# Matmuls of a standing tile of zeros put in front of waiting matmul groups, in a fused attention and mixture-of-experts kernel

## The chip, the core and the metric

The kernel runs on one NeuronCore of a Trainium2 chip. The metric is the device time of one execution in microseconds (us). The engines are named as in the profile: PE is the matmul engine, PEld its weight loads, DVE the vector engine, ACT the scalar engine, POOL GpSimd, SP the engine whose queue issues most transfers. [...]

## The reference

Eight batches, eight heads, 576 positions, head width 64. An attention over 32 memory slots a head gives 4608 token rows of 512; each row then goes through the one expert of eight that its gate picks.

```python
a = softmax(phi)                                   # [B, H, 576, 32]
k_m = einsum('bhsm,bhsd->bhmd', a, k)
v_m = einsum('bhsm,bhsd->bhmd', a, v)
attn = softmax(q @ k_m.T / sqrt(64))
x = (attn @ v_m).transpose(0, 2, 1, 3).reshape(4608, 512)
logits = x @ w_gate
e_idx = argmax(logits); gate_w = softmax(logits)[e_idx]
eom = sigmoid(x @ w_output_gate)
for e in range(8):
    m = e_idx == e
    out[m] = gate_w[m] * eom[m, e] * (relu(x[m] @ w1[e]) @ w2[e])
```

## The kernel before

The attention goes over four pairs of batches (`bp`), and within a pair over five groups of query columns; together 20 groups `g`, worked off in a software pipeline of steps `t`. The list `ORDER` fixes in which order the pieces of a step are written, and every engine runs its own pieces in that order. For a group, PE makes the scores (`scores`, L837, 16 matmuls), DVE transposes them (L847) and takes the maximum (L854), POOL subtracts it (L856), ACT takes the exponential (L860), DVE sums, POOL divides, DVE transposes back (L885), and three steps later PE makes the values (`values`, L898, in two halves of 8 matmuls, called V0 and V1 here; in the last group of a pair there is one half), which ACT copies out (L900, tile `xo`) and SP stores.

Between these pieces lies the work on the memories of the next pair, written out in the lists `MEM0` and `MEM`: transposes of the softmaxed phi (L702), sums of keys and values over positions (L731, tile `pk`, opened and closed by a matmul of a 1-row tile of zeros, L725 and L737), a scaled copy by ACT (L748, `kvm`), its transposes by PE (`turn_kv`, L757), and gates (L771).

When the groups of a pair are done, their tokens are ranked by expert (`rank`): PE adds up ones in a bank of PSUM (tile `pr`, L996 to L1002) that DVE reads (L1005). After the second pair, `route_early` gives the first experts their slots of 576 tokens: a long chain of small DVE operations ends in a comparison (`eqa`, L231), PE turns that into a table of token numbers (`table`, L241, 72 matmuls), DVE copies it out (L248) and makes indices, and POOL gathers the tokens of the first slot (L440, five gathers). Each use of `pr` is a new tile of a pool with one buffer.

Scores and values share the pool `pd` with two buffers of two banks each (tiles `bpd`). A tile that takes a buffer over waits for the last reader of the tile that held it.

The first slot opens in step 17 of the attention: `turn_x` transposes the gathered rows (L1134 in groups of four, L1139 for the last 64 rows), ACT and DVE split them into a high and a low part, and from L1306 on PE works through the experts' products. The rest of the attention is spread over the first two slots. A queue, an order and a buffer for each of these places are fixed when the program is built, except which expert a slot holds.

Of the kernel before, what the change touches and what calls it, by code (L numbers as in the profile page):

```python
# [7 lines left out]
F32 = mybir.dt.float32  # L8
# [45 lines left out]
GROW = ((4, 0, 0), (2, 0, 0), (0, 2, 0))  # L54
SOON = {"pe": 5, "dve": 3, "tab": 20}
PACE = 30
PUMP = (2, 1)
TURN = (12, 14, 16, 17)
TURN6 = (2, 3, 5, 8)
# [23 lines left out]
def attention_moe(tc, phiT, kv, qT, wgo, wall, out):  # L83
# [3 lines left out]
    with contextlib.ExitStack() as ctx:  # L87
# [42 lines left out]
        def iota_f(shape, pattern, base=0, cm=0, name="", dt=F32):  # L130
# [3 lines left out]
            if len(pattern) > 1:  # L134
# [8 lines left out]
                    for nm, n in (("a", NBE), ("l", NBL))}  # L143
# [21 lines left out]
        G.affine_select(out=upto[:], in_=upto[:], pattern=[[1, E], [-1, E]], base=0,  # L165
                        channel_multiplier=0, compare_op=ALU.is_ge, fill=0.0)
        wg = cp.tile([P, H, 16], F32, name="wg")

        ohg = rt.tile([P, NCHT, E], BF16, name="ohg", bufs=1)
        jh = rt.tile([P, NCHT], I32, name="jh", bufs=1)  # L170
# [51 lines left out]
        def table(nm, q, nch, nblk):  # L222
# [11 lines left out]
            yield  # L234
            yield from take_pr()
            yield from hold(LATE["pe"], SOON["tab"])
            pi = ps_r.tile([P, NBL], F32, name="pr")
            for c in range(nch):
                for i in range(2):
                    for r in range(2):  # L240
# [445 lines left out]
        def memory(bp):  # L686
# [65 lines left out]
                                hmask[:].unsqueeze(1).unsqueeze(3).to_broadcast(h2), ALU.mult)  # L752

            def turn_kv(b):
                pt = bank([2, P])
                for g in range(2):
                    T.transpose(pt[:, g], z[b]["kv"][:, g], ident[:])  # L757
                n = 2 * bp + b
                kT = kTp[n % 4]
                z[b]["vT"] = ld.tile([P, 2, P], F32, name="vT_b", bufs=1)  # L760
                for e in range(2):
                    A.copy(kT[64 * e:64 * e + 64], pt[0:64, e].rearrange("p (j m) -> p j m", m=M))
                A.copy(z[b]["vT"][64:128], pt[64:128])
                kTs[n] = kT
# [137 lines left out]
        def rank(bp, lg):  # L902
# [86 lines left out]
            def main():  # L989
                yield from take_pr()  # L990
                yield from hold(LATE["pe"], SOON["pe"])

                route = {1: route_early, NBP - 1: route_late}.get(bp)
                pr = ps_r.tile([P, NCH + 1, E], F32, name="pr")
                if route:
                    T.matmul(pr[:, NCH], ones_b[:], ohcs[bp][:], start=True, stop=True)  # L996
                T.matmul(pr[:, 0:NCH], strict[:], oh, start=True, stop=False)
                if bp:
                    T.matmul(pr[:, 0:NCH], ones_b[:], ohcs[bp - 1][:].unsqueeze(1).to_broadcast(b3),
                             start=False, stop=False)  # L1000
                for c in range(1, NCH):
                    T.matmul(pr[:, c:NCH], ones_b[:], oh[:, 0:NCH - c], start=False, stop=(c == NCH - 1))  # L1002
                yield
                yield from hold(LATE["dve"], SOON["dve"])
                V.tensor_tensor(w1_[:], oh, pr[:, 0:NCH], ALU.mult)  # L1005
                route = route(pr[:, NCH]) if route else iter(())
                next(route, None)
                taken.clear()
                yield
                yield from together(place(), route)  # L1010
# [60 lines left out]
        def turn_x(z, c):  # L1071
# [62 lines left out]
                T.transpose(pt[:, k * P:(k + 1) * P], xg[:, k, c * XQ:c * XQ + P], ident[:])  # L1134
            part(pt, (slice(None), c, slice(0, 512)))
            if c == 0:
                pt = bank([4, 64], "ps")
                for e in range(4):
                    T.transpose(pt[:, e], xg[0:64, 4, e * XQ:e * XQ + P], ident[0:64, 0:64])  # L1139
# [22 lines left out]
        def attention():  # L1162
# [8 lines left out]
            for t in range(NT + LAG["V"]):  # L1171
                for w in ORDER:
# [12 lines left out]
                    elif w == "V0" and 0 <= g < NT:  # L1185
# [3 lines left out]
                        if g == 5 * bp:  # L1189
                            lgs[bp] = rt.tile([P, NCH, 16], F32, name="lg", bufs=2)  # L1190
                        xo = wk.tile([P, 2, 2, 2 * XQ], F32, name="xo", bufs=2)
                        values(bp, 2 * c, st[g], xo)
                    elif w == "V1" and 0 <= g < NT:
                        if c < 4:
                            values(bp, 2 * c + 1, st[g], xo)
                        store(bp, c, xo, lgs[bp])
                    elif w == "C" and 0 < g < NT:
                        while 2 * (g // 5) + (g % 5 >= 2) not in kTs:
                            mem.step()
                        st[g] = scores(g // 5, g % 5)  # L1200
                        if g + NQ < NT:
                            load_q(g + NQ)
# [430 lines left out]
```

## Time and profile before

| | us |
|---|---|
| median of 3 runs | 544.62 (543.31 to 545.51) |
| the profiled execution, its own time | 544.71 |
| its span, first to last instruction | 543.0 |
| PE busy in the span | 503.2 (93%) |
| DVE busy | 370.4 (68%) |
| mean granted clock of PE | 0.953 |

A timeline row gives the start in us from the beginning of the span, the duration, the engine, the line, the operation with output and inputs, the shape, and the number of instructions merged into the row; where the engine was idle ahead of the row, the idle time and what ended it stand in brackets. [...] PE counts as busy while any matmul is under way, at whatever clock.

### The profile page before, as it was taken

The page shows a single profiled execution, that of the slowest core. Times are in us where ns is not written, and L with a number is a line of the kernel's source. Part 1 is how long each engine was busy: PE and PEld are TensorE (multiplying, and loading weights), DVE is VectorE, ACT ScalarE, POOL GpSimd, SP SyncE. Part 2 cuts the span into 40 slices and gives each one's busy share as a digit, 9 for nine tenths or more (in the row PEclk, how much of TensorE's full clock was granted, in tenths as well). Part 3 has the DMA queues.
Part 4 walks back from the last instruction along what each step waited for, and adds up shares of the span by engine and source line. Part 5 has one row for each costly group of instructions (what it writes and reads, how often), then busy time and mean ns, then how long its engine had stood idle before and what let it go on. Part 6 is the DMA issues. An engine that isn't in the chain of part 4 may idle for free. (4 is left out here: it accounts for less than half of the span.)

```text
span 543.0 us, 11086 instructions
## 1 busy us (share of the span) xinstructions
PE 503.2 (93%) x4205; PEld 431.6 (79%) x4205; DVE 370.4 (68%) x804; ACT 282.4 (52%) x543; POOL 170.0 (31%) x176
## 2 busy tenths in 40 slices
PE   3788797849999999999999999999999999999994
PEld 2455565539987799889988998998899899889983
DVE  4374979945982488826484898678779867977600
ACT  4476665254553454225353856576485657648311
POOL 2242645545151151115028223401621241131021
PEclk9977969868999999999999999999999999999998
DMA  8999999795454485217414951880496088120011
GB/s 333 412 397 384 412 385 353 258 344 182 180 167 155 139 235 198 77 73 272 139 37 136 264 174 36 271 244 33 149 263 173 30 267 246 43 94 34 0 45 49
DMA packets 46975, 104.31 MB, mean 192 GB/s; under 512 B 9856, under 2 KB 21440, under 8 KB 46528
## 3 DMA queue, kind: packets, MB, share of 16 engines
q1 hardware_dynamic: 41024, 83.44, 46.5%
q0 software_dynamic: 5888, 20.06, 11.0%
q8 instruction: 35, 0.57, 0.4%
q14 instruction: 28, 0.23, 0.1%
HBM read 77.23 MB, written 20.35 MB: 180 GB/s over the span
## 5 line engine op out<-in xcount | busy, mean ns | idle before, releaser
L1437 PE MATMUL bps<-whl,hh 128*128 128x512 f32 x560 | 167.3, 392 | 0.0
L541 DVE TENSOR_TENSOR whl<-w,whl 128x1024 fp32r<-128x1024 f32 x74 | 90.7, 1234 | 53.4 <-ACT whl L536 52.9
L1437 PEld LDWEIGHTS bps<-whl,hh 128*128 128x128 f32 x560 | 104.5, 188 | 22.0
L1437 PE MATMUL bps<-whl,hl 128*128 128x512 f32 x216 | 84.2, 390 | 0.0
L1306 PE MATMUL bps<-xh,whl 128*128 128x288 f32 x384 | 79.8, 299 | 0.0
L536 ACT CAST whl<-w 128x1024 fp32r<-128x1024 f32 x74 | 76.8, 1049 | 4.1 <-PE bpc L1437 2.7
L1306 PEld LDWEIGHTS bps<-xh,whl 128*128 128x128 f32 x384 | 62.9, 190 | 1.2 <-issue 0.6
L1265 POOL DMA_INDIRECT out<-y,idx_oa x20 | 26.3, 1316 | 102.8 <-ACT y L1264 75.1
L1306 PE MATMUL bps<-xl,whl 128*128 128x288 f32 x192 | 57.0, 297 | 0.0
L1265 POOL DMA_INDIRECT out<-y,idx_ol x20 | 22.3, 1113 | 101.1 <-ACT y L1264 66.6
L1334 PE MATMUL bpc<-xh,whl 128*128 128x288 f32 x240 | 49.5, 295 | 0.0
L1334 PE MATMUL bpc<-th,whl 128*128 128x288 f32 x240 | 49.2, 296 | 0.0
L1437 PEld LDWEIGHTS bps<-whl,hl 128*128 128x128 f32 x216 | 40.6, 188 | 8.1
L1264 ACT ACTIVATE y<-bps,gx 128x512 f32<-128x512 f32 x27 | 18.6, 690 | 44.3 <-PE bps L1437 43.5
L1274 ACT ACTIVATE hh<-bps 128x288 fp32r<-128x288 f32 x48 | 19.7, 411 | 40.4 <-PE bps L1306 40.3
L1334 PEld LDWEIGHTS bpc<-xh,whl 128*128 128x128 f32 x240 | 39.1, 188 | 0.2
L1334 PEld LDWEIGHTS bpc<-th,whl 128*128 128x128 f32 x240 | 38.7, 188 | 0.0
L1274 ACT ACTIVATE hh<-keep 128x288 fp32r<-128x288 f32 x60 | 26.3, 445 | 23.4 <-DVE keep L1345 23.4
L856 POOL TENSOR_TENSOR ea<-ea,mx 128x512 f32<-128x512 f32 (+1 forms) x20 | 19.3, 964 | 58.0 <-DVE mx L854 54.7
L1306 PEld LDWEIGHTS bps<-xl,whl 128*128 128x128 f32 x192 | 36.5, 190 | 0.1
L1334 PE MATMUL bpc<-xl,whl 128*128 128x288 f32 x120 | 35.4, 295 | 0.0
L1334 PE MATMUL bpc<-tl,whl 128*128 128x288 f32 x120 | 35.0, 292 | 0.0
(260 smaller groups left out, 935.0 us busy)
## 6 DMA issues: line engine op xcount, KB each, us to landing
w<-wall SPq DMA_DIRECT2D x64, 512.0 KB, 4.9
kvt<-kv SPq DMA_DIRECT2D x32, 512.0 KB, 7.4
xs<-xo SPq DMA_DIRECT2D x16, 576.0 KB, 6.4
qt<-qT SPq DMA_DIRECT2D x16, 512.0 KB, 9.2
ph<-phiT SPq DMA_DIRECT2D x3, 1152.0 KB, 11.5
xq<-xg SPq DMA_DIRECT2D x40, 80.0 KB, 4.9
xq<-xg SPq DMA_DIRECT2D x40, 64.0 KB, 4.3
kv<-kv SPq DMA_DIRECT2D x4, 512.0 KB, 9.2
```

Of the source, the lines that this page charges most:

```text
L536: A.copy(hl[:, 0], w[:])
L541: V.tensor_tensor(hl[:, 1], w[:], hl[:, 0].bitcast(F32), ALU.subtract)
L856: G.tensor_tensor(eav, eav, mx[:, 0:n].unsqueeze(2).to_broadcast([P, n, M]), ALU.subtract)
L1264: A.activation(y[0:n], py[0:n], AF.Copy, scale=z["g"][0:n, k:k + 1])
L1265: G.indirect_dma_start(out=out, out_offset=bass.IndirectOffsetOnAxis(ap=z["idx"][1][0:n, z["q0"] + k:z["q0"] + k + 1], axis=0), in_=y[0:n] ...
L1274: A.activation(h_[:, j, c:e], src, AF.Relu)
L1306: T.matmul(pb, w[:, b, o:o + P], x[a][:, cc, c * SL // 2:(c + 1) * SL // 2], start=(n == 0), stop=(n == 11))
L1334: T.matmul(pb, w[:, b, o:o + P], z[x][a][:, kc], start=(first and n == 0), stop=(n == 5), skip_group_check=not first)
L1437: T.matmul(py, a, w[:, b, DM * f:DM * f + DM], start=(u == 4 and f == 0 and n == 0), stop=(u == 7 and f == 1 and n == len(ps) - 1))
```

## The change

A tile `still` of 128 x 256 zeros in bf16 is set once by POOL. The function `keep` puts a number of matmuls of it into the second half of the bank that holds the ranks and tables; nothing reads what they write. To that end this bank becomes one standing tile `prs`, of which the ranks and tables use the first columns. `keep` is called ahead of scores (2 matmuls), of each half of the values (1), of the ranks (2), of the table (4) and of the transposes of `kvm` (3), as long as the first slot hasn't opened, and once ahead of L1139 in the first slot (6). The numbers stand in `KEEP`. One hundred such matmuls are issued, each with a weight load of its own.

```diff
--- before.py
+++ after.py
@@ -54,6 +54,7 @@
 GROW = ((4, 0, 0), (2, 0, 0), (0, 2, 0))
 SOON = {"pe": 5, "dve": 3, "tab": 20}
 PACE = 30
+KEEP = {"C": 2, "V": 1, "pr": 2, "tab": 4, "t": 3, "x": 6}
 PUMP = (2, 1)
 TURN = (12, 14, 16, 17)
 TURN6 = (2, 3, 5, 8)
@@ -165,6 +166,14 @@
         G.affine_select(out=upto[:], in_=upto[:], pattern=[[1, E], [-1, E]], base=0,
                         channel_multiplier=0, compare_op=ALU.is_ge, fill=0.0)
         wg = cp.tile([P, H, 16], F32, name="wg")
+        still = rt.tile([P, 256], BF16, name="still", bufs=1)
+        G.memset(still[:], 0.0)
+        prs = ps_r.tile([P, 512], F32, name="prs")
+
+        def keep(key):
+            if "open" not in env or key == "x":
+                for _ in range(KEEP[key]):
+                    T.matmul(prs[:, 256:512], ones_b[:], still[:], start=True, stop=True)
 
         ohg = rt.tile([P, NCHT, E], BF16, name="ohg", bufs=1)
         jh = rt.tile([P, NCHT], I32, name="jh", bufs=1)
@@ -234,7 +243,8 @@
             yield
             yield from take_pr()
             yield from hold(LATE["pe"], SOON["tab"])
-            pi = ps_r.tile([P, NBL], F32, name="pr")
+            pi = prs[:, 0:NBL]
+            keep("tab")
             for c in range(nch):
                 for i in range(2):
                     for r in range(2):
@@ -752,6 +762,7 @@
                                 hmask[:].unsqueeze(1).unsqueeze(3).to_broadcast(h2), ALU.mult)
 
             def turn_kv(b):
+                keep("t")
                 pt = bank([2, P])
                 for g in range(2):
                     T.transpose(pt[:, g], z[b]["kv"][:, g], ident[:])
@@ -991,7 +1002,8 @@
                 yield from hold(LATE["pe"], SOON["pe"])
 
                 route = {1: route_early, NBP - 1: route_late}.get(bp)
-                pr = ps_r.tile([P, NCH + 1, E], F32, name="pr")
+                pr = prs[:, 0:(NCH + 1) * E].rearrange("p (c e) -> p c e", e=E)
+                keep("pr")
                 if route:
                     T.matmul(pr[:, NCH], ones_b[:], ohcs[bp][:], start=True, stop=True)
                 T.matmul(pr[:, 0:NCH], strict[:], oh, start=True, stop=False)
@@ -1134,6 +1146,8 @@
                 T.transpose(pt[:, k * P:(k + 1) * P], xg[:, k, c * XQ:c * XQ + P], ident[:])
             part(pt, (slice(None), c, slice(0, 512)))
             if c == 0:
+                if z["s"] == 0:
+                    keep("x")
                 pt = bank([4, 64], "ps")
                 for e in range(4):
                     T.transpose(pt[:, e], xg[0:64, 4, e * XQ:e * XQ + P], ident[0:64, 0:64])
@@ -1189,14 +1203,17 @@
                         if g == 5 * bp:
                             lgs[bp] = rt.tile([P, NCH, 16], F32, name="lg", bufs=2)
                         xo = wk.tile([P, 2, 2, 2 * XQ], F32, name="xo", bufs=2)
+                        keep("V")
                         values(bp, 2 * c, st[g], xo)
                     elif w == "V1" and 0 <= g < NT:
+                        keep("V")
                         if c < 4:
                             values(bp, 2 * c + 1, st[g], xo)
                         store(bp, c, xo, lgs[bp])
                     elif w == "C" and 0 < g < NT:
                         while 2 * (g // 5) + (g % 5 >= 2) not in kTs:
                             mem.step()
+                        keep("C")
                         st[g] = scores(g // 5, g % 5)
                         if g + NQ < NT:
                             load_q(g + NQ)
```

The order on DVE, ACT and SP is the same in both kernels, and POOL has one more memset. On PE the matmuls are put in between; line numbers after the change are up to 17 higher. The rows below are of PE, from the scores of group 14 on, the last of the third pair (32x64): V0 and V1 of group 11 (each a row of one matmul and a row of three; a row with a wait stands alone), and the sums that follow, up to `pk`. In brackets stand the semaphores waited for, by the engine or the queue that raises them.

Before:

```order
L837 MATMUL bpd<-qt,kT_177 32x64 [waits DMAHW3_49,Activation_49]
L837 MATMUL bpd<-qt,kT_177 32x64 x7
L837 MATMUL bpd<-qt,kT_178 32x64 x8
L898 MATMUL bpd<-ve_b,aT 128x144 [waits DVE_49,Activation_49]
L898 MATMUL bpd<-ve_b,aT 128x144 x3
L898 MATMUL bpd<-ve_b,aT 128x144 [waits Activation_49]
L898 MATMUL bpd<-ve_b,aT 128x144 x3
L725 LDWEIGHTS zero
L725 MATMUL pk<-zero 128x256
```

After:

```order
L848 MATMUL bpd<-qt,kT_180 32x64 [waits DMAHW3_49,Activation_49]
L848 MATMUL bpd<-qt,kT_180 32x64 x7
L848 MATMUL bpd<-qt,kT_181 32x64 x8
L176 LDWEIGHTS ones_b
L176 MATMUL prs<-still,ones_b 128x256
L909 MATMUL bpd<-ve_b,aT 128x144 [waits Activation_49]
L909 MATMUL bpd<-ve_b,aT 128x144 x3
L176 LDWEIGHTS ones_b
L176 MATMUL prs<-still,ones_b 128x256
L909 MATMUL bpd<-ve_b,aT 128x144 [waits DVE_49]
L909 MATMUL bpd<-ve_b,aT 128x144 x3
L735 LDWEIGHTS zero
```

Two things moved. Each group has its matmuls of `still` in front. And V1, the second row with a wait, which waited for ACT (the copy out of V0, whose buffer it took over), now waits for DVE: the pool hands it the other buffer, the one that holds the scores at the head of the rows, and it waits for DVE to have transposed them (L847 before, L858 now). This is the only `bpd` tile of 56 whose buffer differs.

Where that transpose stands on DVE is seen in the rows of DVE after the change; before it they are the same, with the lines L231, L847, L854, L1040, L866, L868, L885 and L248:

```order
L240 TENSOR_TENSOR eqa<-iota_ba,q_1587 128x720 [waits DVE_49]
L858 STREAM_TRANSPOSE ea_186<-bpd 128x8x32 [waits PE_49]
L865 TENSOR_REDUCE mx<-ea_186 128x8 [waits DVE_49]
L1052 TENSOR_REDUCE lg<-xo 128x32 [waits Activation_49]
L877 TENSOR_REDUCE sa<-ea_185 128x16 [waits Activation_49]
L879 RECIPROCAL sa<-sa 128x16 [waits DVE_49]
L896 STREAM_TRANSPOSE aT<-ea_184 128x512 [waits Pool_49]
L258 COPY iv<-prs 128x20 [waits PE_49]
```

The transpose of those scores comes right behind `eqa`, the end of the routing chain, and the copy of the table (`iv`) six rows later; nothing moved here.

The six matmuls of `still` in the first slot stand between the first four transposes (L1134, now L1146) and L1139 (now L1153), which waits for DVE. Besides, the first matmul of `still` behind each reading of the bank by DVE waits for that reading: once after the ranks of the first pair, once after those of the second and once after the table.

## Rows read from the trace of the kernel before

**Rows 1.** Busy time by stretch: start:end, length, engines, granted clock, DMA share, GB/s.

```profile
45.00:51.80 6.80, 6.72 (x96) 4.62 (x96) 2.89 (x7) 3.43 (x9) 1.62 (x2) 0.50 1.00 386
68.80:79.10 10.30, 9.95 (x138) 6.48 (x134) 8.19 (x27) 6.13 (x15) 4.61 (x6) 0.50 1.05 399
79.10:102.20 23.10, 17.39 (x334) 11.92 (x332) 21.29 (x67) 12.36 (x29) 11.52 (x14) 0.93 0.88 296
113.20:126.90 13.70, 10.56 (x79) 8.65 (x80) 8.31 (x14) 8.18 (x18) 4.86 (x6) 0.50 0.68 243
126.90:536.00 409.10, 408.88 (x2654) 367.04 (x2652) 283.44 (x572) 214.36 (x389) 115.25 (x95) 1.00 0.48 144
420.00:430.00 10.00, 10.00 (x46) 8.29 (x45) 8.23 (x12) 7.77 (x12) 1.09 (x2) 1.00 0.06 13
```

**Rows 2.** Timeline of DVE: start, duration, operation; in brackets idle before, releaser.

```profile
52.81 0.72 DVE L847 STREAM_TRANSPOSE ea<-bpd 128x512 f32<-128x512 f32 x1 [3.29 <-PE bpd L837]
...
80.06 0.72 DVE L847 STREAM_TRANSPOSE ea<-bpd 128x512 f32<-128x512 f32 x1 [2.28 <-PE bpd L837]
```

**Rows 3.** Timeline of PE, 43 to 88 us, the same columns.

```profile
43.72 0.64 PE L731 MATMUL pk<-kvt,at 128*32 128x128 f32 x16 [0.64 <-DMA kvt<-kv]
...
65.48 0.46 PE L837 MATMUL bpd<-qt,kT 64*32 64x64 f32 x32 [0.50 <-ACT xo L900]
...
68.31 0.86 PE L898 MATMUL bpd<-ve_b,aT 64*128 64x144 f32 x8 [0.95 <-DVE ea L847]
69.10 0.39 PE L725 MATMUL pk<-zero 1*128 1x256 bf16 x1
69.42 1.94 PE L731 MATMUL pk<-kvt,at 128*32 128x128 f32 x32
...
72.33 1.38 PE L837 MATMUL bpd<-qt,kT 64*32 64x256 f32 x16 [0.35 <-ACT kT L762]
...
74.99 2.29 PE L898 MATMUL bpd<-ve_b,aT 64*128 64x144 f32 x16
...
80.33 1.26 PE L898 MATMUL bpd<-ve_b,aT 64*128 64x144 f32 x16
...
85.91 0.28 PE L725 MATMUL pk<-zero 1*128 1x256 bf16 x1
86.12 1.08 PE L731 MATMUL pk<-kvt,at 128*32 128x128 f32 x32
87.13 0.66 PE L837 MATMUL bpd<-qt,kT 64*32 64x256 f32 x16
```

**Rows 4.** Timeline of DVE, 100 to 105 us.

```profile
100.90 0.91 DVE L231 TENSOR_TENSOR eqa<-iota_ba,q 128x720 bf16<-128x720 bf16 x1
101.72 0.44 DVE L847 STREAM_TRANSPOSE ea<-bpd 128x256 f32<-128x256 f32 x1
...
104.29 0.14 DVE L248 COPY iv<-pr 128x20 f32<-128x20 f32 x1
```

**Rows 5.** Timeline of PE, 97 to 104 us.

```profile
97.79 0.76 PE L898 MATMUL bpd<-ve_b,aT 64*128 64x144 f32 x8 [0.78 <-ACT xo L900]
...
99.70 0.44 PE L757 MATMUL bpa<-ident,kvm 128*128 128x128 f32 x2
101.86 1.36 PE L241 MATMUL pr<-eqa,Aw 128*64 128x20 bf16 x72 [1.72 <-DVE eqa L231]
```

**Rows 6.** Timeline of POOL, 105 to 113 us.

```profile
105.31 1.24 POOL L440 DMA_INDIRECT xg<-xs,idx_ga  x1 [0.32 <-DVE idx_oa L255]
...
111.77 1.06 POOL L856 TENSOR_TENSOR ea<-ea,mx 128x512 f32<-128x512 f32 x1
```

**Rows 7.** Timeline of PE, 113 to 125 us.

```profile
114.47 2.29 PE L898 MATMUL bpd<-ve_b,aT 64*128 64x144 f32 x16
...
121.57 0.68 PE L1139 MATMUL bps<-ident,xg 64*128 64x64 f32 x4 [2.54 <-DVE ea L847]
122.18 2.83 PE L1134 MATMUL bps<-ident,xg 128*128 128x128 f32 x12
```

## The prediction

> **What bounds the kernel now.** I read the busy time by stretch first. From 126.9 us to 536.0, PE is busy 408.88 of 409.10 us at a granted clock of 1.00 [rows 1]: whatever moves the first slot's experts moves the end by as much, and nothing behind 126.9 is touched by the change. So the question is when the first slot gets to its products, and what is worth reading are the stretches ahead of it in which the clock stood at 0.50: 45.0 to 51.8, 68.8 to 79.1 and 113.2 to 126.9 [rows 1] (an earlier one and two shorter ones I leave aside: what PE does before 43.7 is overtaken by a wait for `kvt` [rows 3], and around the short ones DVE sets the pace).
>
> A slow PE costs something only where another engine waits for it. The timeline of DVE shows two such places behind the first two stretches: at 52.81 DVE had waited 3.29 us for scores, at 80.06 another 2.28 [rows 2]. Between 79.1 and 102.2 DVE is busy 21.29 of 23.10 us [rows 1]: there DVE sets the pace, a faster or slower PE changes little, but a chain that enters earlier leaves earlier. It ends with `eqa` (100.90, 0.91 long) [rows 4], the table on PE (101.86, 1.36) [rows 5], its copy on DVE (104.29) [rows 4], and five gathers that hold POOL from 105.31 to 111.77, where the next piece of the attention had stood behind them [rows 6]. Then values at half clock (2.29 us for 16), L1139 after a wait of 2.54 for DVE, twelve transposes in 2.83 [rows 7], and the experts.
>
> **What one matmul of zeros costs.** The trace has no run of them, but two neighbours. A bf16 matmul of 256 columns with its own weights (L725) takes 0.32 us until the next start at half clock (69.10 to 69.42) and 0.21 at full (85.91 to 86.12) [rows 3]; these stand alone. Back to back, 46 matmuls of 512 columns take 10.00 us [rows 1], 0.22 each, so half as many columns 0.11 at full and 0.22 at half clock. The new ones come in ones to fours: I take 0.15 and 0.27, with 0.11 to 0.21 and 0.22 to 0.32 as ends. In a wait that is there anyway they cost nothing.
>
> **Part by part.**
>
> *45 to 52 us.* What the clock is worth: the sums take 1.94 us against 1.08, the values 2.29 against 1.26, the scores 1.38 against 0.66 [rows 3]. This stretch holds one of each kind, so a held clock gives back 0.86 + 1.03 + 0.72 = 2.6. Nine new matmuls stand in it; two fit the wait for `kT` ahead of the scores (0.35 at the same place of the next pair [rows 3]); seven cost 1.05 at full clock, 1.9 at half. Ends: -1.6 if held, +1.9 if not. Before the clock fell at 45, PE waited for chunks of `kvt` (0.64 at 43.72 [rows 3], another just ahead), and no new matmul stands in front of those sums. I take a fall that is shorter than before and pays for the added ones: 0.
>
> *65 to 80 us.* The same pieces with the sums twice: 0.86 more, 3.5, less 1.05 gives 2.4; DVE can use no more than its wait, 2.28 [rows 2]. Ends -2.3 and +1.9. Ahead of the fall at 68.8 PE waited 0.50 at 65.48 and 0.95 at 68.31 [rows 3], and here the new matmuls stand right in front of the groups that waited, five of them and two with the ranks. I take a held clock: -2.3.
>
> [...]
>
> *The second half of the values of group 11.* It ran at 97.79 [rows 5]; now it waits for the transpose of the scores behind `eqa`, which ends at 101.72 + 0.44 = 102.16 [rows 4], and the table stands behind it on PE. Until the table is done PE has to make these 8 matmuls, L725, the sums, three matmuls of zeros, two transposes, four more of zeros, and the table. All at full clock that is 0.63 + 0.21 + 1.08 + 1.05 + 0.44 + 1.36 = 4.8 us [rows 3, 5]; all at half, with everything doubled that has no row, 1.15 + 0.32 + 1.94 + 1.9 + 0.9 + 2.7 = 8.9. PE has nothing to do for some 4 us ahead of it, so I take half clock for the first three (3.4) and full for the rest (2.85): the table ends at 108.4. DVE, which got to the copy at 104.29 [rows 4], copies 0.1 later. So the gathers, and all that stands behind them on POOL, come 4.2 us later against the chain; ends +2.7 and +6.9. It is hidden only if the gathers are not what the first slot waits for; POOL's next piece started as they ended [rows 6], so I count it whole. The two waits of matmuls of zeros for a reading of the bank cost less: the one after the second pair's ranks delays the values of group 10, but that lies in front of the same 4 idle us.
>
> *Values at 114.* At full clock 1.0 less for 2.29 [rows 7], less two matmuls of zeros: ends -0.7 and +0.5. PE waits before them for POOL and ACT, longer than before, with three new matmuls as only cover: 0.
>
> *The first slot.* The six cost nothing in a wait of 2.54 [rows 7] (6 x 0.27 = 1.6); if the wait shrinks, up to 1.6. Held, the clock would halve the 3.5 us of transposes and the 2.2 us of products until 126.9: -2.8; but each transpose goes through ACT and DVE before its product, so -1.6 is what I call the most, 0 the least. I take -0.8.
>
> [...]
>
> *Nothing else.* The memset of POOL lies in the first microseconds; DVE, ACT and SP keep their order.
>
> **Sum.** 0 - 2.3 + 4.2 + 0 - 0.8 = +1.1 us. The profiled execution took 544.71 us, 0.1 above the median; 545.8. A change under 0.5%, 2.7 us, is about what a measurement of this kernel can't tell from none.
>
> **Rivals.**
> - *The clock holds everywhere* (faster): also through 45 to 52 and around the table, values and first slot. -1.6 - 2.3 + 2.7 - 0.7 - 1.6 = -3.5: 541.2. For it: each of the three stretches ends with PE working without a pause, so a little more work may end them sooner. Against it: the 4 us without work ahead of 102, where no matmul of zeros stands.
> - *The clock still falls at 68.8* (slower): the term of 65 to 80 turns from -2.3 into +1.9: 550.0. It decides at the scores at 72: if these take 1.4 us again and not 0.7, this case is there. For it: a matmul of zeros is short beside waits of 0.95.
> - *The late table is hidden*: the first slot waits for ACT and stores instead, and the term of 4.2 is gone: -3.1, 541.6. Against it: POOL [rows 6].
>
> **Chances.** My sum 0.42 (543.3 to 547.6 alone), clock everywhere 0.27, clock falling at 68.8 0.23, hidden table 0.08. The runs before spread over 2.2 us, and the same holds after, so the cases overlap the bound of 2.7 us. Faster by over 0.5%: most of the first and third rival, 0.28; slower: most of the second and the upper part of mine, 0.27; within: 0.45. The range takes in both sides: 540.5 to 550.3.
>
> **What the profile after would show.** V1 of group 11 waiting for DVE some 4 us, and the table starting some 5 us behind the end of `eqa` where it now starts at once; the granted clock at 1.00 between 65 and 80, and DVE's wait of 2.28 gone; gathers some 2 us later than 105.31; the clock at 0.50 again around 102; the products starting at about 126. Wrong would be the prediction if the front gained more than 3 us ahead of `eqa`, if the table's delay were not found at the first slot's start, or if PE had waits behind 130.

## The result

The changed kernel took 550.5 us in the median (548.3, 550.06, 550.95 and 553.59), the kernel before 544.77 on the same chip: a ratio of 1.0109 with an interval of 1.0064 to 1.0154, so 5.9 us slower. The prediction was 545.8 with a range to 550.3. The profiled execution is the fastest of the four (span 546.5 us against 543.0, mean granted clock, as a share of full speed, 0.976 against 0.953), so the profile holds less than the whole loss.

The busy time of the changed kernel by stretch answers [rows 1]; the columns are the same (PE, PEld, DVE, ACT, POOL, granted clock, DMA share, GB/s).

```profile
35.50:45.00 9.50, 8.57 (x170) 5.82 (x168) 6.06 (x13) 6.72 (x14) 3.92 (x5) 1.00 0.92 313
45.00:51.80 6.80, 6.58 (x127) 4.22 (x127) 2.89 (x7) 3.81 (x11) 1.62 (x2) 1.00 0.99 364
68.80:79.10 10.30, 10.17 (x189) 6.76 (x189) 9.37 (x32) 7.69 (x19) 4.50 (x6) 1.00 1.03 406
79.10:93.00 13.90, 11.37 (x192) 7.15 (x192) 12.85 (x36) 7.42 (x17) 8.02 (x12) 1.00 1.02 360
93.20:100.00 6.80, 6.34 (x73) 4.20 (x72) 6.66 (x31) 2.38 (x5) 3.69 (x4) 0.50 1.00 332
110.20:117.00 6.80, 6.13 (x63) 3.37 (x63) 1.05 (x3) 2.43 (x5) 3.66 (x5) 0.50 0.88 333
123.90:127.30 3.40, 3.27 (x17) 3.16 (x18) 2.69 (x7) 1.54 (x3) 1.05 (x1) 0.50 0.54 204
127.30:543.60 416.30, 410.86 (x2662) 368.45 (x2661) 284.34 (x574) 215.06 (x390) 117.84 (x97) 1.00 0.47 142
```

In this execution the clock stood at 1.00 from 35.5 to 93 us, and of the three stretches at 0.50 that the prediction read, the first two are gone. The kernel is slower all the same. DVE, the timeline that answers [rows 2, 4]:

```profile
52.55 0.72 DVE L858 STREAM_TRANSPOSE ea<-bpd 128x512 f32<-128x512 f32 x1 [1.82 <-PE bpd L848]
78.86 0.72 DVE L858 STREAM_TRANSPOSE ea<-bpd 128x512 f32<-128x512 f32 x1 [0.72 <-PE bpd L848]
...
93.39 0.21 DVE L210 TENSOR_TENSOR tge<-prs,thr 128x64 f32<-128x64 f32 x1
...
99.75 0.91 DVE L240 TENSOR_TENSOR eqa<-iota_ba,q 128x720 bf16<-128x720 bf16 x1
100.58 0.44 DVE L858 STREAM_TRANSPOSE ea<-bpd 128x256 f32<-128x256 f32 x1
105.75 0.18 DVE L258 COPY iv<-prs 128x20 f32<-128x20 f32 x1 [2.53 <-PE prs L176]
```

`eqa` comes 1.15 us earlier than in [rows 4], but the copy of the table, which followed it there without a wait, comes 1.46 later, behind a wait of 2.53 for PE. PE in the same stretch and up to the first slot (answers [rows 3, 5, 7]):

```profile
45.09 0.65 PE L741 MATMUL pk<-kvt,at 128*32 128x128 f32 x16 [0.89 <-DMA kvt<-kv]
...
70.97 1.08 PE L741 MATMUL pk<-kvt,at 128*32 128x128 f32 x32
71.98 0.50 PE L176 MATMUL prs<-still,ones_b 128*128 128x256 bf16 x3
72.32 0.38 PE L768 MATMUL bpa<-ident,kvm 128*128 128x128 f32 x2
...
93.66 0.37 PE L176 MATMUL prs<-still,ones_b 128*128 128x256 bf16 x1 [2.35 <-DVE tge L210]
93.96 1.33 PE L909 MATMUL bpd<-ve_b,aT 64*128 64x144 f32 x8
...
101.08 0.76 PE L909 MATMUL bpd<-ve_b,aT 64*128 64x144 f32 x8 [0.66 <-DVE ea L858]
...
104.08 1.31 PE L251 MATMUL prs<-eqa,Aw 128*64 128x20 bf16 x72
...
108.99 0.25 PE L782 MATMUL bpa<-wg,vT_b 64*32 64x16 f32 x9 [1.94 <-issue]
...
113.74 1.01 PE L741 MATMUL pk<-kvt,at 128*32 128x128 f32 x10 [0.67 <-issue]
...
117.56 0.76 PE L909 MATMUL bpd<-ve_b,aT 64*128 64x144 f32 x8
...
124.03 0.69 PE L1153 MATMUL bps<-ident,xg 64*128 64x64 f32 x4 [2.40 <-DVE ea L858]
124.64 2.80 PE L1146 MATMUL bps<-ident,xg 128*128 128x128 f32 x12
127.12 0.46 PE L1323 MATMUL bps<-xh,whl 128*128 128x288 f32 x1
```

The first product of the kernel before, to hold against the last row:

```profile
124.66 0.59 PE L1306 MATMUL bps<-xh,whl 128*128 128x288 f32 x1
```

Read from the top of PE's rows: the sums of the second pair start 1.4 us later than at 43.72 in [rows 3], since PE's work in front of them has grown and their chunks of `kvt` come later. Then the sums take 1.08 instead of 1.94 us. Three matmuls of zeros take 0.34 until the next start. At 93.66 one matmul of zeros holds PE for 2.35 us until DVE has read the ranks, and the clock falls to 0.50 there. V1 of group 11 stands behind the transpose of the scores that follows `eqa` and starts at 101.08 instead of 97.79 [rows 5]; the table starts 3.42 us behind the end of `eqa` (100.66), where before it started at once. POOL's first gather (answers [rows 6]):

```profile
106.43 1.24 POOL L450 DMA_INDIRECT xg<-xs,idx_ga  x1 [2.59 <-DVE idx_oa L265]
...
112.88 1.05 POOL L867 TENSOR_TENSOR ea<-ea,mx 128x512 f32<-128x512 f32 x1
```

The gathers come 1.1 later, the first slot's small transposes 2.46 (124.03 against 121.57), its first product too (127.12 against 124.66).

The 3.5 us between the two profiled executions divide so. The end of `eqa` gives back 1.15. The first gather starts 5.77 us behind that end, where it stood at 3.50 [rows 4, 6]: 2.27 lost. From the first gather to the first product are 20.69 us against 19.35: 1.34 more. Behind the first product come another 1.0; the prediction wanted to see no waits of PE behind 130 us, and the trace after has two there, of 0.4 and 0.3 us.

### The profile page after: what moved, and what is told of

It reads as the page before. It is cut to its first block, busy times and chain, and to the rows that moved or that the text cites. A ratio compares the mean times of both kernels' runs of the same rounds, so it can differ in the third digit from the quotient of the medians.

```text
span 546.5 us, 11285 instructions
## 1 busy us (share of the span) xinstructions
PE 511.8 (94%) x4305; PEld 434.4 (79%) x4305; DVE 368.7 (67%) x804; ACT 282.4 (52%) x543; POOL 171.0 (31%) x177
## 5 line engine op out<-in xcount | busy, mean ns | idle before, releaser
L1323 PE MATMUL bps<-xh,whl 128*128 128x288 f32 x384 | 79.1, 297 | 0.0
L911 ACT COPY xo<-bpd 128x576 f32<-128x576 f32 x36 | 22.9, 639 | 31.6 <-issue 12.6
```

What stands on the lines that cost most here:

```text
L911: A.copy(xo[:, c % 2], px[:, :, 0:2 * XQ])
L1323: T.matmul(pb, w[:, b, o:o + P], x[a][:, cc, c * SL // 2:(c + 1) * SL // 2], start=(n == 0), stop=(n == 11))
```

## The experiments

My theory after the trace was: the late table is the loss, by the moved bank of group 11. Rivals: the wait for `tge`, the matmuls themselves, what they cost ahead of 45 us. Eighteen runs of seventeen kernels follow, each timed beside the kernel before on the same chip; the ratios go by that.

**By place.** `keep` gets the place as a number, and a table `WHERE` says where matmuls are issued; a key that isn't in it keeps all its places.

```diff
-        def keep(key):
-            if "open" not in env or key == "x":
+        def keep(key, n=0):
+            if ("open" not in env or key == "x") and n in WHERE.get(key, ANY):
...
-                        keep("V")
+                        keep("V", 2 * g + int(w[1]))
```

The number is the group for C, twice the group and the half for V, the pair of batches for pr, and the batch for t. The table of each run stands ahead of what was expected of it.

No zeros at all:

```diff
+WHERE = {"t": (), "C": (), "V": (), "pr": (), "tab": (), "x": ()}
```

> No matmul of zeros is issued anywhere; what stays is the one standing tile for ranks and tables, the tile of zeros and its memset. PE's order of matmuls is that of before, but the second half of the values of group 11 still takes the other double bank, so it still waits for the transpose behind eqa. Theory A (the buffer that the standing tile moves is part of the loss): the table starts 1.5 to 2.5 us behind the end of eqa instead of at once, gathers 1.5 to 2.5 us later, 546.3 to 547.3 us. Rival B (all of the loss is the matmuls of zeros themselves, at their places): 544.8 us, that of before, within 0.7. Rival C (the moved buffer is the whole loss): 549 to 551 us.

The front, up to 43 us:

```diff
+WHERE = {"t": (0, 1), "C": (1, 2, 3, 4), "V": (0, 1, 2, 3), "pr": (), "tab": (), "x": ()}
```

> The matmuls of zeros up to 40 us alone (23 of 100). Theory A: the chunks of kvt of the second pair are asked for 1.3 us later (as in the trace after), PE is 1.4 to 1.7 us late at 43.7, and this is overtaken by DVE's wait for scores at 52.8 only if the clock also comes back; here the clock falls at 45 as before, so about 1.5 us reach the ranks of the second pair: 1 to 1.5 us over the kernel with no zeros, 547.5 to 548.5. Rival B (what the front loses is swallowed by the waits of DVE between 52 and 80): the time of the kernel with no zeros, within 0.7.

The middle, 45 to 88 us:

```diff
+WHERE = {"t": (2, 3, 4, 5), "C": range(5, 14), "V": range(4, 20), "pr": (0,), "tab": (), "x": ()}
```

> The matmuls of zeros from 45 to 88 us alone (44 of 100), where in the trace after the clock stood at 1.00 and the shift of PE went from +2.6 to -1.5. Theory A (the gain in the middle is real and only paid away by what stands ahead and behind): eqa ends 1.5 to 3 us earlier than 101.8, the time is 1.5 to 3 us under the kernel with no zeros: 543.5 to 545.5. Rival B (the clock of the middle came from zeros further ahead, or the gain is taken by DVE's pace): the clock falls in 68 to 79 as before, the time is that of the kernel with no zeros plus up to 2 us.

Late, from the second pair's ranks on:

```diff
+WHERE = {"t": (6, 7), "C": range(14, 99), "V": range(20, 99), "pr": (1,)}
```

> The matmuls of zeros from the ranks of the second pair to the first slot alone (33 of 100). Theory A (half of the loss is made here: the matmuls around the table and PE's wait on its own issue at 107 to 109): 2 to 4 us over the kernel with no zeros, 548.5 to 551. Rival B (the wait on issue depends on how many instructions PE has had before, so it is gone when the first 67 are left out): under 1.5 us over the kernel with no zeros, with no wait on issue over 0.5 us in PE between 100 and 120.

Measured: none 1.0002 (0.9982 to 1.0021), front 1.0025 (1.0004 to 1.0047), middle 1.0006 (0.9983 to 1.0028), late 1.0086 (1.0063 to 1.0109). The tables issue 18, 48 and 34 matmuls; the 23, 44 and 33 in the expectations are miscounted. What was expected of the banks in the run without zeros was mistaken: built so, it has the order of matmuls and of banks of the kernel before, and its time. So the standing tile by itself costs nothing that can be told. The front costs about what was expected, though the clock did not fall at 45 us (it was 1.00 from 45 to 51.8); the middle gives nothing, as its Rival B said; and most of the loss sits late, as Theory A said.

The run without zeros shows more: its clock by stretch, to be held against [rows 1].

```profile
45.00:51.80 6.80, 6.40 (x115) 3.88 (x113) 2.89 (x7) 3.56 (x9) 1.62 (x2) 0.75 0.98 364
68.80:79.10 10.30, 8.05 (x171) 5.31 (x167) 10.06 (x32) 7.20 (x18) 4.71 (x6) 1.00 1.03 398
113.20:126.90 13.70, 8.81 (x79) 7.80 (x79) 9.24 (x17) 7.26 (x15) 4.80 (x6) 0.75 0.69 235
```

The same matmuls in the same order, and from 68.8 to 79.1 the clock was 1.00 without a single matmul of zeros, where [rows 1] has 0.50. Where the clock fell between 45 and 127 us was a matter of the execution, not of the program alone. The times say the same: in the 151 executions of the kernel before that stand beside these eighteen runs, the mean granted clock goes from 0.949 to 0.975 with a median of 0.963, and only eight have 0.953, that of the profile read, or less.

**Inside the gap.** From here on the word gap means the 15 zeros from the second pair's ranks to the table.

One, ahead of V1 of group 10:

```diff
+WHERE = {"t": (), "C": (), "V": (21,), "pr": (), "tab": (), "x": ()}
```

> One matmul of zeros in the whole kernel: the one ahead of the second half of the values of group 10, which waits until DVE has read the ranks out of the bank (tge). The buffers are those of before. Theory A (the moved buffer carries the loss): PE waits some 2 us there, which lies in front of the wait for eqa (1.72 us before, 0.75 with no zeros), so 0 to 1 us reach the table: 544 to 545.2. Rival B (this wait alone carries it: values of group 10, scores of 14, values of 11 and the table all go later by it): 2 to 3 us, 546 to 547.

Four, by which the bank moves:

```diff
+WHERE = {"t": (), "C": (14,), "V": (21, 22), "pr": (), "tab": (), "x": ()}
```

> Four matmuls of zeros: the one of the run with one, and those ahead of the scores of group 14 and of the first half of the values of group 11. With them the second half of group 11 takes the other double bank and so waits for the transpose behind eqa, as in the changed kernel. Theory A: the values, the sums and the transposes of the key stand between the end of eqa and the table, 2 to 3 us late against eqa: 546 to 547.3. Rival B (the wait for tge carries it): the same time as with the one matmul. Rival C (both are nothing without the clock and the other zeros): 544.

All but one:

```diff
+WHERE = {"V": tuple(range(21)) + tuple(range(22, 99))}
```

> 99 of the 100: the one ahead of the second half of the values of group 10 is left out, so the wait for tge moves to the zeros ahead of the scores of group 14, two places on, and the second half of group 11 takes its old double bank, so it doesn't wait behind eqa. Theory A: what the table lost is regained, 2 to 3.5 us of the loss of 5.9: 546.5 to 548.5. Rival B (the loss is the number of instructions that PE fetches and issues around 107, or all of the zeros together): 549.5 to 550.5, with the waits on issue (1.9 and 0.7 us) still there.

Middle and slot:

```diff
+WHERE = {"t": (2, 3, 4, 5, 7), "C": (*range(5, 14), 16, 17), "V": (*range(4, 20), 26, 27), "pr": (0,), "tab": (), "x": (0,)}
```

> The zeros from 45 to 88 us as in the run with the middle alone, and those from the turn of the last key to the first slot (19 more); none around ranks, values and table of the second pair, so neither the wait for tge nor the moved buffer. Theory A (all that costs sits between 90 and 106): no more than the middle alone, 543.5 to 544.5, or up to 1.6 less if the six hold the clock over the first slot. Rival B (the zeros ahead of the first slot lengthen PE where it is late): 0.5 to 2 us over the middle alone, 544.5 to 546.

Measured: one 1.0070 (1.0046 to 1.0094), swap 1.0052 (1.0032 to 1.0073), all but one 1.0068 (1.0041 to 1.0095), middle and slot 0.9965 (0.9945 to 0.9986). Four and all but one came out in the times of their Theory A, the second of them for another reason, as the rows below show; middle and slot at the lower end of its Theory A, with 15 matmuls (not 19) added to the middle's 48. A single matmul of zeros cost 3.8 us; by that the theory of the moved bank had fallen and the wait for `tge` had won. But PE's timeline of this run has something that the changed kernel doesn't have:

```profile
123.62 1.12 PE L1148 MATMUL bps<-ident,xg 128*128 128x128 f32 x4 [3.79 <-DVE ea L860]
124.66 0.69 PE L1155 MATMUL bps<-ident,xg 64*128 64x64 f32 x4
```

Here the first four transposes of the first slot wait for DVE, and the small ones follow; in [rows 7] and in the changed kernel it is the small ones that wait, and the four stand long ahead. The banks that the attention leaves are handed out when the program is built, and in this one (as in all but one) the last of them alternate the other way round. So the run measures two things.

**Other bank, no gap, single places.**

All 100, six of them elsewhere (`to` is where `keep` lets them write):

```diff
-        def keep(key):
+        def keep(key, to=None):
...
-                        keep("V")
+                        if g not in (10, 11):
+                            keep("V")
...
             px = banks()
+            if z["k"] in (10, 11):
+                keep("V", px[:, 0, 2 * XQ:512])
...
             sc = banks()
+            if 5 * bp + u == 14:
+                keep("C", sc[:, 0, 256:512])
...
-                        keep("C")
+                        if g != 14:
+                            keep("C")
```

> All 100 matmuls of zeros at their places, but the six ahead of the values of groups 10 and 11 and the scores of group 14 write the free columns of the bank that the next matmuls write anyway (224 columns instead of 256 for the four of the values), not the bank of the ranks. So none waits for tge, and the second half of group 11 takes its old bank. Theory A (the wait for the reading of the ranks makes the table late, and that is the largest part of the loss): the table starts within 1 us of the end of eqa as with all but one, 2 to 3 us under the changed kernel: 547 to 548.5. Rival B (the matmuls themselves, their fetching and their clock carry it): 549.5 to 551.

All but the gap:

```diff
+WHERE = {"t": (0, 1, 2, 3, 4, 5, 7), "pr": (0,), "tab": (), "C": (*range(1, 14), 15, 16, 17), "V": (*range(20), 24, 25, 26, 27)}
```

> 85 of the 100: left out are the 15 from the ranks of the second pair to the table. Theory A (parts add up: front +1.4, middle +0.3, slot -2.2 by the runs with those alone, nothing from the gap): 543.5 to 544.5. Rival B (the front's later chunks of kvt and the later eqa undo what the slot's zeros gave, as in the run with all but one, where the six came on the path): 546 to 547.5.

The six alone:

```diff
+WHERE = {"t": (), "C": (), "V": (), "pr": (), "tab": (), "x": (0,)}
```

> Only the six ahead of the first slot's last four small transposes. Theory A (the zeros of the slot gave the 2.2 us between the middle alone and middle with slot, by a higher clock in the transposes and products): 542.3 to 543.3, with the twelve transposes behind in 1.3 instead of 2.8 us. Rival B (they stand in a wait of 2.5 to 3.4 us and change nothing; the 2.2 came from elsewhere): 543.7 to 544.3.

The seven at the table:

```diff
+WHERE = {"t": (6,), "C": (), "V": (), "pr": (), "tab": (0,), "x": ()}
```

> Only the seven around the turn of the key ahead of the table. Theory A: they take 0.8 us at full and 1.5 at half clock and stand in front of a wait for eqa of 0.75 to 1.7 us; 544 to 545, the table starting at most 0.7 behind the end of eqa. Rival B (there is no slack ahead of the table): 545 to 546.5.

Measured: six in their own bank 1.0047 (1.0022 to 1.0072), all but the gap 1.0004 (0.9981 to 1.0028), the six 0.9982 (0.9955 to 1.0008), the seven 0.9993 (0.9968 to 1.0018). So, taken together, the other 85 cost nothing, and the loss comes with the gap's 15; the seven of them that stand nearest to the table don't cause it by themselves (Theory A). The six alone lie between their two theories and can't be told from no change. The run with six elsewhere has the table on time and a time within its Theory A, but again the first transposes wait for DVE, so it is not clean.

**Banks written down.** The last open point: wait, moved bank and the banks of the first slot apart. The two buffers become two pools, and a row of digits says which is next.

```diff
-        env["pd"] = pso.enter_context(tc.tile_pool(name="pd", bufs=2, space=PSUM))
+        env["pd"] = [pso.enter_context(tc.tile_pool(name="pd" + i, bufs=1, space=PSUM)) for i in "46"]
+        turns = iter("46464646464646464646464646464646464666464646")
...
+            if isinstance(pd, list):
+                pd = pd["46".index(next(turns))]
```

These are the turns of before; those of the changed kernel have a 4 at the 37th place. The row of before goes into the run with one, into the change, and into the run with six elsewhere; that of the changed kernel into the run without zeros.

The wait alone:

> The one matmul of zeros that waits for tge, with each double bank written down in the order of before (the run with one had got another order behind group 11, by which the first transposes of the first slot waited for DVE). So the wait is the only thing added. Theory A (the wait alone makes the table late): the table starts 2 to 4 us behind the end of eqa, 546 to 547.3 us. Rival B (the wait is swallowed ahead of eqa and the 3.8 us of the run with one were the banks of the first slot): 543.5 to 545.

The moved bank alone:

> No matmul of zeros at all; the double banks in the order of the changed kernel, so that the second half of the values of group 11 waits for the transpose behind eqa. That is the prediction's late table by itself. Theory A (it costs by itself as much as predicted, with values, sums and transposes of the key behind the end of eqa): the table 2.5 to 3.5 us behind the end of eqa, 546 to 548. Rival B (it only bites where the wait for tge is there as well): 543.5 to 544.5.

The change with the banks of before:

> The whole change, all 100, with the double banks in the order of before. Theory A (either of the two, the wait for tge or the moved bank, makes the table late, and both together little more than one): the table still 2 to 3 us behind the end of eqa, 547.5 to 550. Rival B (the moved bank is what makes the table late once the clock is held): the table at the end of eqa, 543.5 to 545.

All 100 without wait and moved bank:

> All 100 matmuls, the six around the values of groups 10 and 11 in the free columns of the next matmuls' own bank, and the double banks in the order of before: neither the wait for tge nor a moved bank is left, only the matmuls. Theory A (the matmuls cost what the run without the gap's 15 cost): 543 to 544.5. Rival B (the matmuls in the gap cost by themselves, as the run without the fixed order may suggest): 545.5 to 547.

Measured: the wait alone 1.0028 (0.9999 to 1.0057), the moved bank alone 1.0049 (1.0023 to 1.0075), all with the banks of before 1.0049 (1.0020 to 1.0079), all with neither 1.0016 (0.9987 to 1.0044). PE with the wait alone, and DVE:

```profile
93.26 0.37 PE L178 MATMUL prs<-still,ones_b 128*128 128x256 bf16 x1 [2.59 <-DVE tge L212]
...
103.99 2.10 PE L253 MATMUL prs<-eqa,Aw 128*64 128x20 bf16 x72
```

```profile
99.36 0.91 DVE L242 TENSOR_TENSOR eqa<-iota_ba,q 128x720 bf16<-128x720 bf16 x1
...
106.13 0.18 DVE L260 COPY iv<-prs 128x20 f32<-128x20 f32 x1 [3.31 <-PE prs L253]
```

PE with the moved bank alone, and then with all 100 but neither:

```profile
99.24 1.33 PE L915 MATMUL bpd<-ve_b,aT 64*128 64x144 f32 x8 [5.32 <-DVE ea L864]
103.31 2.10 PE L253 MATMUL prs<-eqa,Aw 128*64 128x20 bf16 x72
```

```profile
100.26 1.31 PE L252 MATMUL prs<-eqa,Aw 128*64 128x20 bf16 x72 [1.35 <-DVE eqa L241]
```

Each of the two makes the table late by itself, 3.7 and 4.5 us behind the end of `eqa`; without both, PE waits for `eqa` again. But the two don't add up. PE, DVE and POOL of the change with the banks of before:

```profile
94.84 0.37 PE L176 MATMUL prs<-still,ones_b 128*128 128x256 bf16 x1 [2.23 <-DVE tge L210]
...
102.18 0.76 PE L913 MATMUL bpd<-ve_b,aT 64*128 64x144 f32 x8 [0.57 <-ACT xo L915]
...
105.18 1.31 PE L251 MATMUL prs<-eqa,Aw 128*64 128x20 bf16 x72
...
123.12 0.46 PE L1157 MATMUL bps<-ident,xg 64*128 64x64 f32 x4 [2.40 <-DVE ea L862]
...
125.22 0.59 PE L1327 MATMUL bps<-xh,whl 128*128 128x288 f32 x1
```

```profile
100.93 0.91 DVE L240 TENSOR_TENSOR eqa<-iota_ba,q 128x720 bf16<-128x720 bf16 x1
```

```profile
107.53 1.24 POOL L450 DMA_INDIRECT xg<-xs,idx_ga  x1 [2.52 <-DVE idx_oa L265]
```

V1 of group 11 waits for ACT here, as in the kernel before, and it still starts 0.34 us behind the end of `eqa`, the table 3.34 and the first gather 5.69. In the changed kernel, where V1 waits for DVE, these are 0.42, 3.42 and 5.77. Behind the wait for `tge` the moved bank has 0.08 us left to add.

From none to all, by the times: the matmuls 0.16%, the wait 0.33% more (1.0049 less 1.0016), the moved bank 0.60% more (1.0109 less 1.0049). Wait and bank together are 0.93%, 5.1 us of the 5.9 measured, with an interval of some 2.9 either way; that they carry the larger part of the loss is shown. How the 5.1 divides between them is not: the interval of the 0.33 reaches 0.41 either way, that of the 0.60 reaches 0.54 (there are only four executions of the changed kernel), and the traces don't give the 0.60 to the table. In the two profiles the first product comes 23.38 and 26.46 us behind `eqa`; of these 3.1 us, 2.0 lie between the first gather and the small transposes, and 1.0 behind these. There the changed kernel has a second wait of PE in "issue" (0.67 us at 113.74) and half clock from 110.2 to 117 and from 123.9 on. Whether that belongs to the bank or to the execution, no run here separates. Nor does a run write the banks down and change nothing else; that all but the gap, with one pool, lost nothing either speaks against a cost of the two pools.

By their expectations, the wait alone and the moved bank alone came out as Theory A (the table of the second later than it said), the change with the banks of before with the late table of its Theory A and a time just below it, and all with neither has the table on time and a time between its two theories. The banks of the first slot alone are the difference between one with and without written turns, 0.42%, and between six elsewhere with and without, 0.31%, each with an interval of 0.38% either way; in the traces the first product comes 27.89 against 24.79 and 25.99 against 22.60 us behind `eqa`.

**The part that pays.** The best run once more, and the slot alone:

```diff
+WHERE = {"t": (7,), "C": (16, 17), "V": (26, 27), "pr": (), "tab": (), "x": (0,)}
```

The repeat:

> The same program as the run with middle and slot, once more on another call. If its 0.35% is real: 0.995 to 0.998 of before. If it was the best of many draws: 0.998 to 1.002.

The slot:

> Only the slot's 15 (turn of the last key, values of group 13, scores of 16 and 17, and the six). Theory A (the gain sits at the first slot, the middle gives nothing): 0.995 to 0.998 of before, the first product up to 2 us earlier than 124.7. Rival B (it needs the clock that the middle's zeros hold): 0.999 to 1.002.

Measured: 0.9955 (0.9934 to 0.9976) and 0.9988 (0.9965 to 1.0012). Middle and slot together beat the kernel before twice, by 0.35 and 0.45%; either alone can't be told from no change, and why the two give more together is not shown. The run with the slot alone decides for neither of its theories. Of 100 matmuls the 63 of this version are the ones worth having.

## Why the prediction was wrong

Three steps of the prediction failed, and the largest is that of 65 to 80 us. It took -2.3 for a held clock, from a stretch at 0.50 and a wait of DVE that belonged to one execution; the timed run with the middle's zeros alone gave +0.3. The wait for the ranks, taken at nothing, makes the table late by itself. And the front, left aside, costs 1.4.

All twenty profiles on one page, from their timelines: the end of `eqa`; the starts of the table, of the first gather and of the first product behind it; the first product in the span; and the span (us).

```
run                 eqa ends  table  gather  product behind  product at  span
before                101.81   0.05    3.50           22.85      124.66 543.0
none                  100.57   0.05    3.50           23.79      124.36 544.0
front                 102.32   0.05    3.51           22.60      124.92 544.1
seven at table        101.66   0.05    3.49           23.20      124.86 543.5
middle                 99.94   0.05    3.50           22.45      122.39 541.6
six                    99.97   0.21    3.50           22.76      122.73 540.3
slot                   98.40   0.05    3.51           21.11      119.51 538.5
middle, slot          100.50   0.05    3.49           21.93      122.43 540.8
middle, slot (2)       98.03   0.05    3.51           21.27      119.30 538.1
all but gap           100.48   0.05    3.49           22.01      122.49 540.2
all, neither          100.21   0.05    3.50           22.60      122.81 540.5
wait alone            100.27   3.72    6.55           24.79      125.06 543.0
moved alone            98.83   4.48    7.30           26.37      125.20 542.9
all, old banks        101.84   3.34    5.69           23.38      125.22 543.8
four (swap)            99.82   4.48    7.30           26.62      126.44 546.1
late                   99.97   5.03    7.39           27.88      127.85 547.3
changed kernel        100.66   3.42    5.77           26.46      127.12 546.5
all, six elsewhere    100.88   0.05    3.50           25.99      126.87 544.5
all but one           102.22   0.05    3.50           26.00      128.22 547.4
one                    99.86   3.74    6.56           27.89      127.75 547.0
```

*What bounds the kernel: right.* The span is the first product plus 417.6 to 419.7 us in all twenty. What moves the first slot moves the end, give or take 1 us.

*The late table: right in its place, too large in its size.* The gathers were forecast 4.2 later against the chain (2.7 to 6.9); in the changed kernel they come 2.27 later (5.77 less 3.50). The sum had the first three pieces at half clock, behind some 4 idle us; in the changed kernel V1 of group 11 waited only 0.66 us for DVE, and PE was at 1.00 from 100 to 110 us. With the moved bank alone PE makes them at 0.50, the gathers come 3.80 later, and the time grows by 2.7 us (1.3 to 4.1).

*The step on the wait for the ranks: wrong.* "The one after the second pair's ranks delays the values of group 10, but that lies in front of the same 4 idle us." It was taken at nothing. By itself it brings the gathers 3.05 later (6.55) and costs 1.5 us, at the edge of the noise (-0.1 to 3.1); in the change the table is late by it with either order of the banks. The slack ahead of the table was not 4 us: it is the 1.72 in front of the table [rows 5], while the 0.78 in front of V1 of group 11 is a wait for ACT's copy, which moves with the values. A wait of 2.35 there, and the clock at 0.50 from 93.2 to 100 behind it (92.7 to 96.2 in the kernel before), are more than that. The matmul of zeros at 93.66 writes the second half of the bank, and these 2.35 us end when DVE has read the ranks in the first (`tge`).

*65 to 80 us, -2.3: wrong, and the largest miss.* The clock held, as forecast, and DVE's wait shrank from 2.28 to 0.72. But it holds without the zeros too. In the ten other profiles of kernels without zeros there, the clock from 68.8 to 79.1 stood at 0.97 to 1.00, and DVE waited at most 0.89 us for scores that it transposed between 74 and 82 us. In the run without zeros, for one, it didn't wait at all:

```profile
77.60 0.70 DVE L860 STREAM_TRANSPOSE ea<-bpd 128x512 f32<-128x512 f32 x1
```

So the 2.28 belonged to one execution. Over the profiles without the front's zeros, `eqa` ends at 100.1 in the mean of ten without the middle's zeros (98.4 to 101.8) and at 99.5 in the mean of three with them: some 0.6 and not 2.3, within the spread; by its time the middle alone is 1.0006, +0.3 us (-0.9 to 1.5). A part of what a faster PE wins it waits for at the end. PE with the middle alone, ahead of the second pair's ranks:

```profile
89.05 0.64 PE L743 MATMUL pk<-kvt,at 128*32 128x128 f32 x16 [1.37 <-DMA kvt<-kv]
```

Before, PE had no wait for `kvt` at this place; without zeros it was 0.67, and each of the nineteen other profiles has one between 86 and 92 us. DMA shows a share of 1.00 and 1.05 in the first two rows of [rows 1], and 0.99 to 1.03 in the stretches of after from 45 to 93 us.

*Ahead of 43.7, left aside: wrong.* "What PE does before 43.7 is overtaken by a wait for `kvt`." The wait itself comes later (45.09 against 43.72): the front alone costs 0.25%, 1.4 us (0.2 to 2.6), and over the profiles above `eqa` ends 1.26 later in the mean of seven with the front's zeros than of thirteen without.

*Values at 114, taken at 0: open.* In the changed kernel they ran at full clock (0.90 us from one half to the next, at 117.56), but behind sums and scores at 0.50.

*The first slot, -0.8: about right by itself, not seen in the change.* With the slot's six or 15 zeros and neither wait nor moved bank the first product comes 21.1 to 22.8 us behind `eqa`, without them 22.4 to 23.8: 1.0 less in the mean. By their times the six alone and the 15 alone can't be told from nothing. In the changed kernel the stretch from the first gather to the first product didn't shrink but grew, by 1.34.

*The price of a matmul: right.* 0.15 was taken, with 0.11 to 0.21 as ends; in the changed kernel three in a row take 0.11 each at full clock.

With the measured sizes the sum is +1.4 for the front, +0.3 for the middle, +5.1 for wait and bank and -1.0 for the slot: 5.8, measured 5.9. That is less of a proof than it looks: the 5.1 is itself a part of the 5.9, the intervals of the parts reach 1 to 3 us either way, and middle and slot together gave more than the two alone. The rival that came nearest in time, "the clock still falls at 68.8", 550.0, is not what happened: the clock stood at 1.00 there, and at the scores of 73 us, where it was to decide, they take 0.87 us until the next start and not 1.4.

Open is what turns gathers that come 2.3 later into a loss of 5.1: the profile of the changed kernel, its fastest execution, shows 1.3 between them and the first product and 1.0 behind it, and its slower executions have no trace.

## What to carry to other kernels

A stretch at half clock in one profile can be a draw and no property of the program (here 0.50 from 68.8 to 79.1 in the profile of before, 1.00 in that of the run without zeros, with the same order of matmuls): before it becomes a term, look at a second execution, and ask whether another engine or a transfer takes the time that a faster PE would win. Work that keeps an engine busy is still an instruction in its queue: ask of each one what it waits for (here one waited 2.35 us for DVE to read the other half of the bank that it writes), and what stands behind it. And where buffers are handed out when the program is built, compare their order before and after an edit and write it down in an experiment, or two effects are measured as one.

## What the hardware showed that was not expected

In 11 of the 20 profiles PE stood for 0.2 to 1.9 us a piece in "issue", with nothing to wait for that the trace shows, between 104 and 117 us: 1.94 and 0.67 in the changed kernel, 0.84, 0.31 and 0.20 in the run without zeros, whose order is that of before, which shows none. So it too can differ between executions of one order, and it was not traced to a cause.

More clock was worth little here. Up to 535 us the clock was at 0.50, with all 100 and neither wait nor moved bank, only from 28.3 to 35.1 and from 110.2 to 120.5 us; with the middle's 48 alone from 28.0 to 34.8, 45.1 to 48.5, 99.7 to 106.5 and 116.8 to 123.6. The times of the two, 1.0016 and 1.0006 of before, can't be told apart.
